# Layer two with the token units outside and the weight sets inside, result sums kept in SBUF, and late weights made one pass earlier

## The chip, the core and the metric

The kernel runs on one core of one Trainium2 chip. The metric is the device time of one execution in microseconds (us). Five engines work side by side, each on its own stream of instructions: PE (TensorE, matmul; PEld is its weight load), DVE (VectorE), ACT (ScalarE), POOL (GpSimd) and SP (SyncE, which here only issues DMAs). ACT and POOL issue DMAs too; such an issue stands in the engine's own stream, so an instruction behind it comes after it. SBUF is the on-chip memory of the engines, PSUM the accumulators of PE, and DRAM everything else.

## The reference

Attention over pooled keys and values, and two gated layers on the 4608 rows of 512 that come out of it. Everything is float32.

```python
def _attn_ref(q, k, v):                 # 8 x 8 heads, 576 long, 64 wide; k and v are means of 8 rows
    scores = scale * np.matmul(q, k_p.transpose(0, 1, 3, 2))
    scores = scores - np.max(scores, axis=-1, keepdims=True)
    attn = np.exp(scores)
    attn = attn / (np.sum(attn, axis=-1, keepdims=True) + 1e-09)
    return np.matmul(attn, v_p).astype(np.float32)

def _moe_ref(x, w_in, w_out):           # "layer one": 4608 x 512, d_ff 2048
    h = x @ w_in
    g = h * (1.0 / (1.0 + np.exp(-1.702 * h)))
    return (g @ w_out).astype(np.float32)

def _moe2_ref(x, w_a, w_b, w_out):      # "layer two": d_ff 1536
    a = x @ w_a
    b = x @ w_b
    return (a * b @ w_out).astype(np.float32)
```

## The kernel before

**Numbers in two halves.** Each float32 factor is split into a rounded part hi and a rest lo, and a product is three matmuls: hi by hi, hi by lo, lo by hi. A split is a copy on ACT (hi) and a subtraction on DVE (lo).

**Blocks, units, passes.** The 4608 tokens are nine blocks of 512. Passes 0 and 1 (attention and the first ten d_ff chunks of layer one) run block by block. From pass 2 the blocks go in five units: units 0 to 3 are two blocks each, unit 4 is the ninth block alone, in two halves of 256. Pass 2 is layer one's last pass; its units come in the order 4, 0, 1, 2, 3. Passes 3, 4 and 5 are layer two: 12 d_ff chunks f in three sets of weights of four chunks, called A, B and C here. From pass 2 each chunk of a unit is made with seven products of half-size matrices in place of eight (`PRODUCTS`), so each unit needs seven operands (three are quarters of the input, `RAW`, and four are differences of quarters, `MIXED`).

**A turn.** A turn is one set of one unit: four chunks of seven products, each of six matmuls (line 784, 168 in all), with a few ACT copies (lines 794 to 798) and DVE steps (from line 800) on each chunk's banks, then the sweep: 14 groups of six matmuls (line 907, 84 in all) that multiply by w_out and whose sums are added into the result (`add_out`: line 954 for a first sum, 956 for the others). A turn's groups run among the next turn's products; `TABLES` says after which product (the O entries). Of a unit of two blocks a matmul has 512 columns, of unit 4 it has 256.

**Order of the turns.** Sets outside, units inside: A0 A1 A2 A3 A4, B0 to B4, C0 to C4 (`steps`, line 1037). The next unit's operands are therefore loaded at each turn, and the sums of a unit leave and come back between its sets:

- Operands. Layer one's result is turned into seven operands (`operand_steps`), all split into hi and lo, that go to DRAM (`yd`, 1 MB each for a unit of two blocks). For units 2 and 3 of pass 2 these steps go one for each product (`PACED`, `results`), for the others all at once. In layer two, `product` issues the load of the next unit's operand (line 417, `load_operand`) on ACT's queue as soon as the last product that reads the old one has been written; the load waits there until the buffer is free. The first unit of a set is loaded by SP.
- Sums. In sets A and B each sum goes to `part[2]` in DRAM, and in B and C it is read back (`load_quarter`, the L entries of `TABLES`, on SP).
- Weights. A set is 28 pieces of w_a and w_b (`wc`, 256 KB each) and 14 of w_out (`wo`, 256 KB each); it is loaded once, by SP.

**Making the weights.** Each chunk of w_a and w_b (a key f) and each pair of chunks of w_out (a key o) is read, combined into seven mixtures, split and stored to DRAM (`wd`) by some tens of small instructions. The first five f keys and three o keys are made in pass 1. The other ten keys (f 5 to 11 and three o) are made in layer two, from A0 to the start of B4 (`made_late`, `pieces_late`): loads and stores on POOL's queue (lines 1224 and 1238), casts on ACT (lines 1134 and 1235), sums on DVE (lines 1135 to 1157, 1236), in tiles called spare and v.

A scheduler puts the instructions of each engine in order from the order in which the code issues them and from their dependences; `tc.issue_after` pins one behind another.

## Time and profile before

| | us |
|---|---|
| median of three runs | 1751.64 |
| lowest and highest of them | 1748.36, 1755.93 |
| the profiled execution | 1749.56 |
| span of its instructions | 1747.7 |
| PE busy | 1700.7 (97%) |
| DVE busy | 1232.7 (71%) |
| ACT busy | 747.3 (43%) |
| POOL busy | 165.7 (9%) |

All steps below are made on the profiled execution, whose time is 1.9 us above its span and 2.1 us below the median. The mean granted TensorE clock was 0.994. The span divides by PE's first product (line 784) of each part: attention and passes 0 and 1 up to 634 us, pass 2 from 634 to 897 us, then the fifteen turns of layer two, A0 from 897 to 956 us and C4 last. A row of the profile names line, engine, operation and tiles (out<-in); the bracket at the end is the idle time of the engine just before, and what ended it.

### The profile page before, as it was taken

To read this page: it belongs to the slowest core of one execution; us is meant where nothing else is said; L and a number is where in the kernel's file an instruction comes from. 1 tells how busy PE (TensorE), PEld (TensorE's weight loads), DVE (VectorE), ACT (ScalarE), POOL (GpSimd) and SP (SyncE) were. 2 spreads that over 40 slices of the span, in tenths; PEclk is the share of its full clock that TensorE was granted. 3 is DMA by queue.
4 is the path that set the end of the run, shared out by engine and by line. 5 is a ranking of instruction groups with operands and counts; after the bars stand their busy time and mean duration, and the time that the engine had idled before them with its cause. 6 is when DMAs were issued, how large, how long until landed. Compare 5 with 4: busy or idle time off the path is not lost.

```text
span 1747.7 us, 24378 instructions
## 1 busy us (share of the span) xinstructions
PE 1700.7 (97%) x8672; PEld 1417.9 (81%) x8672; DVE 1232.7 (71%) x2251; ACT 747.3 (43%) x1782; POOL 165.7 (9%) x282
## 2 busy tenths in 40 slices
PE   9999999999999999999999999999899899999998
PEld 8888887878888888788887777888778787788887
DVE  8999866675868745656637777786778765566666
ACT  8976643543334435455433443443333322222222
POOL 0000000010100001113212211111111100000000
PEclk9999999999999999999999999999999999999999
DMA  7776466465978985476698567499685678734543
GB/s 293 247 270 240 177 209 228 157 229 208 374 276 309 403 320 196 170 272 231 227 403 294 223 259 263 162 358 328 268 331 185 250 270 324 294 126 187 217 157 109
DMA packets 135641, 438.87 MB, mean 251 GB/s; under 512 B 15520, under 2 KB 31392, under 8 KB 114656
## 3 DMA queue, kind: packets, MB, share of 16 engines
q1 hardware_dynamic: 100544, 281.32, 44.5%
q0 software_dynamic: 22880, 78.92, 12.3%
q10 hardware_dynamic: 12096, 77.08, 11.1%
q8 instruction: 68, 1.11, 0.3%
q14 instruction: 53, 0.43, 0.1%
HBM read 291.24 MB, written 146.01 MB: 250 GB/s over the span
## 4 chain that ended last, share of the span: by engine, by line
PE 71%; DMA 11%; DVE 9%; issue 4%; ACT 3%; POOL 1%; SPq 0%; ACTq 0%; POOLq 0%; DVEq 0%
PE X L784 16%; PE acc L907 11%; PE Y L784 8%; PE acc L325 4%; PE acc L326 4%; PE acc L327 4%; PE h L325 4%; PE Z L784 4%; PE h L326 4%; PE h L327 4%; PE acc L715 3%; PE acc L716 3%; PE acc L717 3%; DMA xo<-yd 2%; DMA part<-ys 1%
## 5 line engine op out<-in xcount | busy, mean ns | idle before, releaser
L784 PE MATMUL X<-xo,wc 128*128 128x512 f32 (+1 forms) x1800 | 419.4, 373 | 22.8 <-ACT s L794 10.0
L784 PEld LDWEIGHTS X<-xo,wc 128*128 128x128 f32 x1800 | 319.0, 190 | 86.8 <-ACT s L794 11.1
L784 PE MATMUL Y<-xo,wc 128*128 128x512 f32 (+1 forms) x900 | 210.2, 369 | 5.0 <-DMA xo<-yd 2.5
L784 PEld LDWEIGHTS Y<-xo,wc 128*128 128x128 f32 x900 | 158.4, 188 | 35.5 <-ACT s L796 3.3
L306 ACT CAST ghi<-s 128x512 fp32r<-128x512 f32 (+1 forms) x137 | 79.9, 583 | 243.2 <-PE acc L907 194.8
L907 PE MATMUL acc<-ghi,wo 128*128 128x512 f32 (+1 forms) x548 | 179.1, 372 | 2.0 <-DVE part L956 2.0
L325 PE MATMUL h<-x,w 128*128 128x512 f32 x360 | 144.0, 401 | 2.7 <-ACT x L604 2.2
L326 PE MATMUL h<-x,w 128*128 128x512 f32 x360 | 141.2, 392 | 0.5 <-DVE x L606 0.5
L327 PE MATMUL h<-x,w 128*128 128x512 f32 x360 | 141.1, 392 | 0.0
L326 PE MATMUL acc<-glo,w 128*128 128x512 f32 x360 | 140.3, 390 | 0.2 <-DVE glo L1392 0.2
L327 PE MATMUL acc<-ghi,w 128*128 128x512 f32 x360 | 140.4, 390 | 0.0
L956 DVE TENSOR_TENSOR part<-acc,part 128x512 f32<-128x512 f32 (+1 forms) x170 | 104.9, 634 | 45.8 <-PE acc L907 40.7
L307 DVE TENSOR_TENSOR glo<-s,ghi 128x512 fp32r<-128x512 f32 (+1 forms) x137 | 87.7, 640 | 67.0 <-ACT ghi L306 66.7
L325 PE MATMUL acc<-ghi,w 128*128 128x512 f32 x360 | 131.1, 398 | 0.4 <-ACT ys L1414 0.4
L907 PEld LDWEIGHTS acc<-ghi,wo 128*128 128x128 f32 x548 | 101.9, 189 | 20.6 <-issue 1.9
L794 ACT COPY s<-X 128x512 f32<-128x512 f32 (+1 forms) x75 | 40.8, 543 | 173.5 <-PE X L784 145.1
L784 PE MATMUL Z<-xo,wc 128*128 128x512 f32 (+1 forms) x450 | 105.2, 369 | 0.9 <-DMA xo<-yd 0.7
L907 PE MATMUL acc<-glo,wo 128*128 128x512 f32 (+1 forms) x274 | 101.9, 372 | 0.0
L560 ACT ACTIVATE at<-sc,mx 128x72 f32<-128x72 f32 x288 | 88.2, 341 | 27.5 <-DVE mx L553 27.3
L907 PE MATMUL acc<-hi,wo 128*128 128x512 f32 (+1 forms) x292 | 94.9, 372 | 3.3 <-ACT spare L1235 2.1
L996 POOL DMA_DIRECT2D yd<-st x126 | 67.7, 541 | 269.0 <-ACT st L306 229.4
L784 PEld LDWEIGHTS Z<-xo,wc 128*128 128x128 f32 x450 | 79.7, 189 | 15.8 <-DVE s L814 1.1
(133 smaller groups left out, 3155.2 us busy)
## 6 DMA issues: line engine op xcount, KB each, us to landing
xo<-yd ACTq DMA_DIRECT2D x63, 1024.0 KB, 10.2
part<-part SPq DMA_DIRECT2D x128, 256.0 KB, 3.9
yd<-st POOLq DMA_DIRECT2D x126, 256.0 KB, 3.1
xo<-yd SPq DMA_DIRECT2D x21, 1024.0 KB, 8.3
part<-part SPq DMA_DIRECT2D x19, 1024.0 KB, 8.6
xd<-x SPq DMA_DIRECT2D x18, 1024.0 KB, 7.4
xm<-xd SPq DMA_DIRECT2D x32, 512.0 KB, 8.3
xo<-xd SPq DMA_DIRECT2D x12, 1024.0 KB, 7.7
```

Of the source, the lines that this page charges most:

```text
L306: nc.scalar.copy(out=hi, in_=src)
L307: (nc.vector.tensor_tensor(out=lo, in0=src, in1=f32(hi), op=ALU.subtract))
L325: nc.tensor.matmul(out=o, lhsT=whi, rhs=xhi, start=first, stop=False),
L326: nc.tensor.matmul(out=o, lhsT=whi, rhs=xlo, start=False, stop=False),
L327: nc.tensor.matmul(out=o, lhsT=wlo, rhs=xhi, start=False, stop=last),
L560: pin("ACT", nc.scalar.activation(out=a[:, h, :], in_=sc[:, c, :], func=AF.Exp, bias=mx[:, h:h + 1], accum_out=sm[:, h:h + 1],))
L715: after_last(nc.tensor.matmul(out=oa, lhsT=whi, rhs=chi, start=first, stop=False))
L716: after_last(nc.tensor.matmul(out=oa, lhsT=wlo, rhs=chi, start=False, stop=False))
L784: after_last(nc.tensor.matmul(out=banks[nm], lhsT=w[we][:, ks], rhs=x[:, xe, kk, :], start=n in FIRST and kk == 0 and m == 0, stop=kk == 1 ...
L907: after_last(nc.tensor.matmul(out=o_, lhsT=w_, rhs=x_, start=n in FIRST and k_ % 2 == 0 and m == 0, stop=k_ % 2 == 1 and m == 2, skip_grou ...
L956: nc.vector.tensor_tensor(out=t, in0=a, in1=t, op=ALU.add)
L996: nc.gpsimd.dma_start(out=yd[u][:, o, e, kk] if w_ == N else yd[u][:, o, e], in_=f32(ts[e]))
```

## The change

- **Order of the turns.** Units outside, sets inside, forwards and backwards in turn: A0 B0 C0, C1 B1 A1, A2 B2 C2, C3 B3 A3, A4 B4 C4 (`turns`, `after`). Ten of the fourteen steps from turn to turn change the set, four change the unit.
- **Operands** are loaded once for each unit, by SP, each pinned behind the one before (`last_x`), in place of once in each turn on ACT's queue. Only the three quarters are stored in two halves (1 MB); the four differences are stored unsplit (`ym`, 0.5 MB) and split in layer two by `split_operand`: two in the last chunk of the unit before (behind products 2 and 4), two in the first chunk (behind products 6 and 3).
- **Weights** are loaded anew at each change of set: eleven times in all. The `wc` pieces of chunk n are issued on SP one chunk ahead of the use of their slot, starting in the second chunk of the turn before; the `wo` pieces on POOL's queue within the sweep (the first set's on SP).
- **Sums** of a unit stay in four `part` tiles and one tile of tag wo through its three sets; only the finished ones are stored to the output.
- **Layer one's result.** The steps that make operands come two for each product for all units. A unit of two blocks takes 14 DVE instructions (8 differences, 6 splits) and 6 casts on ACT, in place of 22 and 14.
- **Making of the late weights.** Nine keys (f 6 to 11, three o) in place of ten, begun with pass 2: `tick`, called for each product, issues a share of them over 147 products, of which 105 are pass 2's and 42 the first turn and a half of layer two's; each is pinned behind the last anchored copy or sum. The sixth f key is made in pass 1, and the first two keys (f 0 and o 0) move from pass 1 into the last block of pass 0.
- **Layout.** `wd` holds all hi parts of a key before its lo parts; stores take longer runs, loads two pieces. In pass 2 the second `part` tile takes a slot of tag w in place of v, and SP issues the `part` loads ahead of the operands.

```diff
...
+    turns = []
+    for u in range(NU2):
+        sets = list(range(LP, L2))
+        turns += [(i, u) for i in (sets if u % 2 == 0 else sets[::-1])]
+    after = dict(zip(turns, turns[1:]))
...
-    yd = [dram.tile([P, 7, 2, 2, N if len(u) == 2 else HALF], F32, name=f"yd{n}") for n, u in enumerate(units)]
+    yd = [dram.tile([P, 3, 2, 2, N if len(u) == 2 else HALF], F32, name=f"yd{n}") for n, u in enumerate(units)]
+    ym = [dram.tile([P, 4, 2, N if len(u) == 2 else HALF], F32, name=f"ym{n}") for n, u in enumerate(units)]
...
-    wd = {f: dram.tile([P, 7, 2, 2 * P], F32, name=f"wd{f}") for f in range(NF2)}
+    wd = {f: dram.tile([P, 2, 7, 2 * P], F32, name=f"wd{f}") for f in range(NF2)}
...
-        2: [dram.tile([P, KD, N], F32, name=f"part2_{j}") for j in range(NB)],
...
+        x_t[operand_key(i, u, o)] = t
+        if o in RAW and i >= LP:
             src = yd[u][:, o]
...
+        elif i >= LP:
+            t, src = t[:, 1], ym[u][:, o - 3]
...
-        (queue or nc.sync).dma_start(out=f32(t), in_=src)
+        with tc.issue_after(last_x[0]) if i >= LP and u > 0 else nullcontext():
+            made = nc.sync.dma_start(out=f32(t), in_=src)
+        last_x[:] = [made.ins]
...
-        t = part_t.pop((i, u, col_n, c)) if i < FINISHES else part_t[j][:, c, cols]
+        t = part_t[j][:, c, cols]
...
-            for o in results[:1]:
+            for o in results[:2]:
                 o()
-            del results[:1]
+            del results[:2]
+            tick()
...
-            if last:
-                x_t.pop((i, u, o))
-                if not one_ and u + 1 < NU2:
-                    load_operand(i, u + 1, USED.index(o), nc.scalar)
...
+        ahead = {}
+        if first and (one_ or (i, u) == turns[0]):
+            ahead = {"": (u, 3), "P1": (u, 4), "P6": (u, 5), "P3": (u, 6)}
+        elif first and u != before_[i, u][1]:
+            ahead = {"P6": (u, 5), "P3": (u, 6)}
+        elif last and not one_ and (i, u) in after and after[i, u][1] != u:
+            ahead = {"P2": (u + 1, 3), "P4": (u + 1, 4)}
...
-            if u == NU2 - 1 and i + 1 < L2 and k_ in (3, 7, 11, 13):
-                load_o(i + 1, k_ // 4)
+            if not final and after[i, u][0] != i and k_ in (3, 7, 11, 13):
+                load_o(after[i, u][0], k_ // 4, nc.sync if (i, u) == turns[0] else nc.gpsimd)
...
-            t = part_t[i, u, c, col] = out_tile(c, col, cols.stop - cols.start)
+            n_ = cols.stop - cols.start
+            if col:
+                if (u, "half") not in part_t:
+                    part_t[u, "half"] = big("wo", [P, KD, n_], F32, "sums")
+                t = part_t[u, "half"][:, c]
+            else:
+                t = p2.tile([P, n_], F32, tag="part", name="sum", bufs=4)
+            part_t[u, c, col] = t
...
-        if done:
...
+        if done and after.get((i, u), (0, NU2))[1] != u:
+            part_t.pop((u, c, col))
+            ended.append(op(
+                nc.sync.dma_start, out[c * P:(c + 1) * P, j * N + cols.start:j * N + cols.stop], t
+            ))
...
+        ts = [spare(list(part_.shape), F32R, "st") for _ in range(2)]
...
-        def step(o, out_, a, b, kk):
-            if a is not None:
-                sub(out_, a, b, kk)
-            split_store(u, o, out_, kk)
...
-        todo_ = [(0, b11, None, None), (1, b21, None, None), (2, b22, None, None), (3, b11, b12, b11),
-                 (5, b12, b22, b12), (4, b22, b22, b11), (6, b21, b21, b22)]
-        return [op(step, *x, kk) for x in todo_ for kk in range(2 if b11.shape[-1] == N else 1)]
...
+            return a[:, kk] if wide else a
+        def mixture(o, a, b, kk):
+            a, b = (t[x, kk] if isinstance(x, int) else cut(x, kk) for x in (a, b))
+            t[o, kk] = spare(list(a.shape), F32, "mix")
+            nc.vector.tensor_tensor(out=t[o, kk], in0=a, in1=b, op=ALU.subtract)
+            nc.gpsimd.dma_start(out=ym[u][:, o - 3, kk] if wide else ym[u][:, o - 3], in_=t[o, kk])
+        ks = range(2 if wide else 1)
+        def chained(kk):
+            mixture(3, b12, b11, kk)
+            mixture(4, b22, 3, kk)
+            mixture(6, b21, 4, kk)
+        todo_ = [(chained,), (mixture, 5, b22, b12), (split_store, u, 2, b22), (split_store, u, 0, b11),
+                 (split_store, u, 1, b21)]
+        return [op(*x, kk) for kk in ks for x in todo_]
...
-        steps_ = operand_steps(u, *q4)
-        if u in PACED:
-            results.extend(steps_)
-        else:
-            for o in steps_:
-                o()
+        results.extend(operand_steps(u, *q4))
...
-    steps = [(i, j, f) for i in range(len(passes)) for j in order[i] for f in chunks(i, j)]
+    steps = [(i, j, f) for i in range(LP) for j in order[i] for f in chunks(i, j)]
+    steps += [(i, u, f) for i, u in turns for f in passes[i][1]]
...
-    HELD, EARLY = FM - FA, FB + 1
+    HELD, EARLY = FM - FA, FB + 2
...
+    def tick():
+        if not background:
+            return
+        pace[0] += 1
+        while background and background[0][0] <= pace[0]:
+            _, o = background.pop(0)
+            with ExitStack() as pinned:
+                for ins in anchored.values():
+                    pinned.enter_context(tc.issue_after(ins))
+                o()
+    def in_background(ops, ticks):
+        total, done = sum(o.cost for o in ops), 0.
+        for o in ops:
+            background.append((2 + ticks * done / total, o))
+            done += o.cost
...
-    spread_late(mixed_x(3) + made_p(2), place[0, J9, 1], place[0, J9, FM - 1])
+    spread_late(mixed_x(3) + made_p(2) + made([0]), place[0, J9, 1], place[0, J9, FM - 1])
     J5 = order[1][-1]
     spread_late(
-        mixed_x(4) + made(range(EARLY)),
+        mixed_x(4) + made(range(1, EARLY)),
...
-    spread_late(
-        made_late(range(EARLY, NF2)), place[LP, 0, passes[LP][1][1]], place[L2 - 2, NU2 - 1, passes[L2 - 2][1][0]] - 3,
...
+    for u, next_ in zip(order[i], order[i][1:] + [None]):
+        homes = ("wo", "w") if len(units[u]) == 2 else ("w",)
+        parts = [op(load_part, j, t) for j, t in zip(units[u][::-1], homes)]
+        if next_ is not None:
+            before.setdefault((i, u, fs[1]), []).extend(parts + operands(i, next_))
...
+            before.setdefault((i, u, fs[0]), []).extend(parts + loads(LP))
+    before[LP, 0, passes[LP][1][1]] = [op(load_o, LP, m, nc.sync) for m in range(4)]
+    for (i, u), (i2, u2) in after.items():
+        fs, fs2 = passes[i][1], passes[i2][1]
+        if u2 != u:
+            before.setdefault((i, u, fs[-1]), []).extend(operands(LP, u2))
+        if i2 != i:
+            for n, f in enumerate(fs2):
+                key = (i, u, fs[n + 1]) if n + 1 < FB else (i2, u2, fs2[0])
+                before.setdefault(key, []).extend(ab_ops(i2, f))
...
```

ACT at a change of unit in layer two, before (B0 to B1; xo is an operand and yd1 its place in DRAM, s a chunk's sums, hi and ghi rounded halves, v a weight being made):

```order
L798 COPY s_11363<-X_11324 128x512
L954 COPY part_11368<-acc_10946 128x256
L306 CAST hi_11407<-s_11218 128x512
L954 COPY part_11373<-acc_10950 128x256
L306 CAST ghi_11434<-s_10936 128x512
L417 DMA xo_11390<-yd1_92 128x2048
L417 DMA xo_11403<-yd1_92 128x2048
L417 DMA xo_11417<-yd1_92 128x2048
L417 DMA xo_11430<-yd1_92 128x2048
L794 COPY s_11461<-X_11452 128x512
L796 COPY s_11469<-Y_11453 128x512
L1134 ACTIVATE v_11180<-spare_11188 128x256
```

and now (C0 to C1):

```order
L804 COPY s_10135<-Y_10113 128x512
L806 COPY s_10143<-X_10112 128x512
L311 CAST hi_10176<-s_10014 128x512
L311 CAST ghi_10199<-s_9785 128x512
L435 CAST xo_10100<-xo_10100 128x1024
L435 CAST xo_10102<-xo_10102 128x1024
L802 COPY s_10212<-X_10203 128x512
L804 COPY s_10220<-Y_10204 128x512
L311 CAST ghi_10231<-s_10014 128x512
L806 COPY s_10241<-X_10203 128x512
L311 CAST hi_10253<-s_9913 128x512
L435 CAST xo_10106<-xo_10106 128x1024
```

The four loads that stood between a turn's last cast and the next turn's first copy `s` are gone from ACT; two casts that split operands of the next unit stand there instead, and two more behind the first copies.

SP in set B, before (`part` are sums in SBUF, part2 their place in DRAM):

```order
L612 DMA part2_0_134<-part_11380 128x512
L612 DMA part2_0_134<-part_11382 128x512
L947 DMA part_11685<-part2_0_134 128x512
L947 DMA part_11687<-part2_0_134 128x512
L612 DMA part2_1_135<-part_11420 128x512
L612 DMA part2_1_135<-part_11422 128x512
L947 DMA part_11800<-part2_3_137 128x512
L947 DMA part_11802<-part2_3_137 128x512
L612 DMA part2_1_135<-part_11297 128x512
L612 DMA part2_1_135<-part_11299 128x512
L947 DMA part_11918<-part2_3_137 128x512
L947 DMA part_11920<-part2_3_137 128x512
```

and now, in unit 1's turns (wc is a set's weights, wd their place in DRAM):

```order
L1305 DMA wc_10620<-wd7_113 128x2x1024
L1305 DMA wc_10735<-wd0_106 128x2x1024
L1305 DMA wc_10737<-wd0_106 128x2x768
L1305 DMA wc_10737<-wd1_107 128x2x256
L1305 DMA wc_10849<-wd1_107 128x2x1024
L1305 DMA wc_10851<-wd1_107 128x2x512
L1305 DMA wc_10851<-wd2_108 128x2x512
L1305 DMA wc_10957<-wd2_108 128x2x1024
L1305 DMA wc_10959<-wd2_108 128x2x256
L1305 DMA wc_10959<-wd3_109 128x2x768
L1305 DMA wc_11051<-wd3_109 128x2x1024
L430 DMA xo_11377<-ym2_98 128x1024
```

The stores and loads of sums are gone from SP, and loads of weights stand there, with the next unit's operands behind them.

DVE in pass 2, before, where a unit's operands are made (part is layer one's result, st a half to be stored, glo a rest):

```order
L800 TENSOR_TENSOR s_6969<-s_6969,Y_6897 128x512
L730 TENSOR_TENSOR part_6686<-acc_6977,part_6686 128x512
L767 TENSOR_TENSOR glo_6996<-s_6969,ghi_6995 128x512
L307 TENSOR_TENSOR st_7082<-part_6686,st_7081 128x512
L1001 TENSOR_TENSOR part_6686<-part_6680,part_6686 128x512
L809 TENSOR_TENSOR s_6949<-s_6949,X_6896 128x512
L1001 TENSOR_TENSOR part_6680<-part_6680 128x512
L307 TENSOR_TENSOR st_7100<-part_6680,st_7099 128x512
L730 TENSOR_TENSOR part_6686<-acc_7011,part_6686 128x512
L767 TENSOR_TENSOR glo_7027<-s_6949,ghi_7026 128x512
L1001 TENSOR_TENSOR part_6680<-part_6680,part_6686 128x512
L307 TENSOR_TENSOR st_7088<-part_6686,st_7087 128x512
```

and now (v and raw are a weight being made):

```order
L808 TENSOR_TENSOR s_7149<-s_7149,Y_7070 128x512
L1138 TENSOR_SCALAR v_6932<-v_6932 128x256
L1137 TENSOR_SCALAR v_6932<-v_6932 128x256
L1141 SCALAR_TENSOR_TENSOR v_6932<-raw_6977,v_6932 128x256
L1138 TENSOR_SCALAR v_6932<-v_6932 128x256
L1144 TENSOR_SCALAR raw_6977<-v_6932 128x256
L1141 SCALAR_TENSOR_TENSOR v_6932<-raw_7033,v_6932 128x256
L743 TENSOR_TENSOR part_6779<-acc_7157,part_6779 128x512
L1145 SCALAR_TENSOR_TENSOR raw_6977<-raw_6977 128x256
L778 TENSOR_TENSOR glo_7180<-s_7149,ghi_7179 128x512
L1144 TENSOR_SCALAR raw_7033<-v_6932 128x256
L1148 TENSOR_TENSOR v_6932<-v_6932,raw_6977 128x256
```

Between the same two steps of a chunk (lines 800 and 767 before, 808 and 778 now), where one sum stood, stand that sum and seven small instructions that make weights.

## Rows read from the trace of the kernel before

**Rows 1.** Page: busy time, share of the span, instructions of each engine.

```profile
PE 1700.7 (97%) x8672; PEld 1417.9 (81%) x8672; DVE 1232.7 (71%) x2251; ACT 747.3 (43%) x1782; POOL 165.7 (9%) x282
```

**Rows 2.** Turns A1 to B3, C0 to C2: start:end, length, busy (instructions), clock, DMA share, GB/s.

```profile
core 0: us, PE busy (x) PEld busy (x) DVE busy (x) ACT busy (x) POOL busy (x), PEclk, DMA share, GB/s
955.61:1022.47 66.86, 60.10 (x253) 48.08 (x253) 46.98 (x101) 25.43 (x48) 11.41 (x19) 0.97 0.66 249
1022.47:1079.62 57.15, 57.15 (x254) 47.30 (x252) 46.56 (x97) 24.88 (x46) 13.64 (x21) 1.00 0.62 225
1079.62:1140.64 61.02, 58.05 (x254) 46.93 (x252) 44.72 (x97) 23.85 (x45) 9.25 (x15) 1.00 0.62 231
1140.64:1180.16 39.52, 39.52 (x253) 35.91 (x252) 32.82 (x76) 19.19 (x41) 7.63 (x12) 1.00 0.97 359
1180.16:1229.40 49.24, 48.76 (x254) 41.50 (x253) 35.71 (x82) 18.12 (x42) 7.64 (x12) 1.00 0.92 337
1229.40:1297.66 68.26, 61.25 (x254) 49.37 (x252) 52.47 (x108) 20.88 (x40) 14.19 (x22) 0.95 0.71 267
1297.66:1360.03 62.37, 57.90 (x253) 47.06 (x252) 48.96 (x102) 20.04 (x37) 8.71 (x14) 1.00 0.69 255
1360.03:1418.70 58.67, 57.83 (x253) 47.07 (x252) 43.80 (x76) 17.64 (x31) 5.47 (x8) 1.00 0.63 233
...
1458.61:1512.82 54.21, 50.10 (x255) 42.66 (x253) 26.62 (x54) 11.99 (x25) 0.00 (x0) 0.97 0.74 278
1512.82:1575.04 62.22, 59.07 (x254) 48.39 (x252) 38.13 (x59) 15.76 (x27) 0.00 (x0) 0.97 0.54 202
1575.04:1632.16 57.12, 57.12 (x254) 47.30 (x252) 36.80 (x57) 15.35 (x26) 0.00 (x0) 1.00 0.53 200
```

**Rows 3.** The same view of pass 2, and of 50 us near pass 0's end.

```profile
634.18:897.43 263.25, 262.37 (x1282) 222.03 (x1281) 154.61 (x236) 133.48 (x232) 53.03 (x99) 1.00 0.65 239
...
455.00:505.00 50.00, 50.00 (x223) 41.38 (x222) 33.75 (x63) 19.72 (x30) 2.65 (x4) 1.00 0.85 323
```

**Rows 4.** Timeline of ACT at the change from B0 to B1: start, length, instruction.

```profile
1224.75 10.99 ACTq L417 DMA_DIRECT2D xo<-yd  x4
1235.78 0.58 ACT L794 COPY s<-X 128x512 f32<-128x512 f32 x1 [10.59 <-DMA wo<-wdo]
```

**Rows 5.** Timeline of PE at the same place.

```profile
1230.77 1.52 PE L784 MATMUL Y<-xo,wc 128*128 128x512 f32 x6
...
1236.42 1.43 PE L784 MATMUL X<-xo,wc 128*128 128x512 f32 x4 [2.78 <-ACT s L794]
```

**Rows 6.** Timeline of ACT at two steps of the late weights.

```profile
1289.35 0.41 ACT L1235 CAST spare<-v 128x256 fp32r<-128x256 f32 x1 [4.51 <-DMA wdo<-spare]
...
1356.33 0.43 ACT L1134 ACTIVATE v<-spare 128x256 f32<-128x256 f32 x1 [5.30 <-DMA spare<-in_moe_w_a_dram]
```

**Rows 7.** Timeline of PE at three such places.

```profile
1251.28 0.47 PE L907 MATMUL acc<-hi,wo 128*128 128x512 f32 x1 [2.06 <-ACT spare L1235]
...
1290.43 0.50 PE L784 MATMUL Y<-xo,wc 128*128 128x512 f32 x1 [2.18 <-ACT s L796]
...
1358.54 0.73 PE L784 MATMUL X<-xo,wc 128*128 128x512 f32 x2 [3.58 <-DVE s L814]
```

**Rows 8.** Turns A1 to B4: all work on tile v, then line 1143 alone.

```profile
core 0: us, DVE busy (x) ACT busy (x) POOL busy (x), PEclk, DMA share, GB/s
955.61:1458.61 503.00, 103.30 (x280) 39.26 (x80) 27.27 (x40) 0.99 0.72 268
...
955.61:1458.61 503.00, 16.60 (x40) 0.99 0.72 268
```

**Rows 9.** Groups by line: busy, mean ns | idle before them, and what ended it.

```profile
L1235 ACT CAST spare<-v 128x512 fp32r<-128x512 f32 (+1 forms) x40 | 22.5, 568 | 30.1 <-DMA wdo<-spare 9.3 <-DMA wd<-spare 8.2 <-DVE v L1146 6.6
L1134 ACT ACTIVATE v<-spare 128x256 f32<-128x256 f32 x40 | 17.0, 434 | 26.4 <-DMA spare<-in_moe_w_out_dram 7.5 <-DMA wd<-v 6.5 <-DMA spare<-in_moe_w_a_dram 6.0
L1236 DVE TENSOR_TENSOR v<-v,spare 128x512 fp32r<-128x512 f32 (+1 forms) x40 | 24.2, 619 | 8.7 <-ACT spare L1235 8.4
L422 DVE TENSOR_TENSOR xo<-xo 128x1024 fp32r<-128x1024 f32 (+1 forms) x20 | 22.3, 1116 | 19.0 <-ACT xo L421 19.0
L421 ACT CAST xo<-xo 128x1024 fp32r<-128x1024 f32 (+1 forms) x20 | 19.3, 964 | 11.4 <-DMA xo<-xc 11.3
```

**Rows 10.** DMA issues: count, KB each, median us from issue to landing.

```profile
xo<-yd SPq DMA_DIRECT2D x21, 1024.0 KB, 8.3
...
wc<-wd SPq DMA_DIRECT2D x12, 1024.0 KB, 12.2
...
xo<-xc SPq DMA_DIRECT2D x16, 512.0 KB, 6.5
```

221 lines of the change are left out of this document (86 added, 135 removed), and 6 rows, old and new, of tables (ENDING, TABLES).

## The prediction

> **What bounds the kernel now.** I read the page first: PE is busy 97% of the span [rows 1], so nothing is won by making another engine faster as such; only idle time of PE, or its matmuls, can shorten the run. The change keeps all matmuls of layer two. So the question is where PE loses time and whether the change touches it. Next I cut layer two at PE's first product of each turn [rows 2]. In C2 PE is busy for the whole 57.12 us: that is the floor of a turn of a unit of two blocks with a wide sweep behind it. B0, with unit 4's narrow sweep in it, has 49.24 us and C0 should have the same; A4, narrow products with a wide sweep, takes 39.52 us with PE never idle. Against these floors the turns lose: A1 66.86 - 57.12 = 9.74; A2 nothing; A3 61.02 - 57.12 = 3.90; B1 68.26 - 57.12 = 11.14; B2 62.37 - 57.12 = 5.25; B3 58.67 - 57.12 = 1.55; C0 54.21 - 49.24 = 4.97; C1 62.22 - 57.12 = 5.10. Together 41.65, with the small rests of the turns not shown some 42 us. Pass 2 loses nothing that matters: 262.37 of 263.25 us busy [rows 3]. So the most that the change can win in layer two is 42 us, and everything that it adds can only take from that.
>
> **What causes the 42 us.** The third view is the timeline at the costliest place, B0 to B1. Four issues of operand loads stand in ACT's queue and take 10.99 us there, for each waits until the old operand's buffer is free; the copy of the first product's bank, which PE needs to go on, stands behind them, and ACT starts it only after 10.59 us of idleness, at 1235.78 [rows 4]. PE's next products follow it at 1236.42, 2.78 us idle [rows 5]. The bracket names a DMA of wo as the releaser, but the row above it says what ACT was doing. A second cause stands in B1 to B3: casts of the late weights wait 4.51 and 5.30 us on ACT for a DMA [rows 6], and what stands behind them reaches PE late, 2.06 + 2.18 + 3.58 = 7.8 us [rows 7]. So I put about 34 us down to the operand loads on ACT and 8 to the late weights.
>
> **The change, part by part.** All from the profiled 1749.56.
>
> *Operand loads leave ACT: minus 34 us.* The waiting issues go from ACT altogether; on SP they wait too, but nothing that PE needs at once stands behind them there except weights that are wanted about three quarters of a turn later. There are four changes of unit in place of twelve inside the sets.
>
> *What a change of unit costs now.* An operand's buffer is free when its last product ends. A product or a group is six matmuls; 252 of them take 57.12 us, so one takes 0.227 and six 1.36. In the last chunk the first product is followed by six more products and two groups, 8 x 1.36 = 10.9 us, before the next unit's first product wants its operand; 1 MB on SP lands in 8.3, 0.5 MB in about 6.5 [rows 10], and the operands that come unsplit need a cast and a subtraction more, 0.96 + 1.12 = 2.1 us [rows 9]. It fits by 1 to 3 us, if SP issues at once. Lower bound zero: A2 and C2 took seven whole operands without loss [rows 2]. Upper bound 5.1 each: C1, where no late weights are made. The four changes of set C lost 5.1, 0, 0 and next to nothing, 1.4 in the mean; I take 1.0, since 5 MB come in place of 7 and ACT is free: 4 x 1.0 = plus 4 us (0 to 20).
>
> *Ten changes of set.* Each brings 10.5 MB of weights. A load lands 12.2 us after its issue [rows 10], and it is issued three chunks ahead, 3/4 of 57.12 = 43 us; 11.0 million bytes in 57.12 us are 193 GB/s, where A4 ran at 359 [rows 2]. What is taken away is larger: per turn 7 MB of operands and the sums, both ways. I cost the changes at nothing; the cover is those 43 us. If it fails, the price is C0's, the one change of set that lost: 4.97 each (0 to 50).
>
> *Unit 4's turns.* B4 has narrow products and a narrow sweep: 39.52 - (57.12 - 49.24) = 31.6 us. The set for C4 has to come in this time: 11.0 million bytes at 359 GB/s are 30.7 us, at B1's 267 they are 41.2. Between 0 and 41.2 - 31.6 = 9.6 late; I take 2, near the first, since nothing else is loaded there.
>
> *Late weights, now mostly in pass 2.* In layer two the ten keys took 103.30 + 16.60 = 119.9 us of DVE and 39.3 of ACT [rows 8]; nine are 108 and 35. 105 of the 147 products over which they are spread are pass 2's: 71%, 77 us of DVE and 25 of ACT. The units of two blocks save 8 DVE instructions each, 32 x 0.62 (line 1236's 512 columns [rows 9]) = 20 us. DVE in pass 2 goes to 154.6 + 77 - 20 = 212 of 263 us, 80%, ACT to some 155. A2 had DVE at 46.56 of 57.15, 81%, with late weights in it and no loss [rows 2]. So the load is carried; what stays is waits at the head of a queue. What is queued behind such a wait on ACT are the copies of banks X and Y and the casts of the gate's halves, and PE waits for these. Lower bound 0; upper bound all of ACT's idle time before the two lines, (30.1 + 26.4) x 9/10 = 50.9 us [rows 9], if none of it were hidden. Before, 7.8 us of it reached PE for ten keys, 0.78 each; I take the same for nine, plus 7, since the instructions and their waits are the same and now pinned behind the copies instead of ahead of them.
>
> *Sums in SBUF, layout, early keys.* The sums' stores and loads were on SP and nobody waited for them in C2; with them gone the adds cost as before: 0. The sixth f key goes to passes 0 and 1 and two move into pass 0's last block; at its end PE is never idle with DVE at 33.75 of 50.00 us [rows 3], so one key (12 us of DVE) is covered: plus 1 (0 to 7.8, the three stalls of rows 7). In pass 2 five units' operand steps come two for each product, 14 instructions in place of 22: hidden as before, 0.
>
> **Sum.** 1749.56 - 42 + 4 + 0 + 2 + 7 + 1 = 1721.6. The profiled execution lies 2.1 below the median of 1751.64, so 1723.7, say 1723.
>
> **Rivals.**
>
> R1, *the stalls belong to the transfers, not to ACT's queue.* Then moving the issue wins little at the four changes that are left, and they cost what inside-set changes cost before, from 2.4 us (the mean of A1 to A4's and C1 to C4's, 19.1/8) to 5.1. For it: the profile's bracket names a DMA [rows 4]. Against it: the copy waits for no DMA's data, and C2 took 7 MB with no loss. It gives 1721.6 + 4 x 1.4 = 1727 up to 1721.6 + 4 x 4.1 = 1738. The Trainium skill, in "DMA: Bandwidth & Descriptors", section "Issuing engines are not separate DMA queues", says that DMAs issued by scalar, sync or gpsimd run on the same 16 engines and that spreading the issue saves only the sequencer's time to initiate, usually small. By that rule the move from ACT to SP would win nearly nothing of itself; the row of 10.99 us for four issues disagrees, because the wait for a free buffer is the sequencer's time too.
>
> R2, *slower: the head-of-line waits of the late weights are exposed in pass 2.* The mechanism is one: a cast of a late weight waits on ACT (or DVE) for its DMA while copies of product banks stand behind it, in a pass that before lost nothing and where DVE goes from 59% to 80%. Price up to 50.9. With all of it exposed 1723 - 7 + 51 = 1767. It decides from the point at which 7 + 28 + 8.7 = 44 us are exposed (slower by over 0.5%, which is 8.7 us and about what a measurement can tell); from 27 us on the gain is within 0.5%.
>
> R3, *the last unit becomes bound by DMA*: B4 and C4 each wait the 9.6 us worked out above: 1723 - 2 + 2 x 9.6 = 1740.
>
> R4, *slower: sets arrive late at every change of set* because SP's or POOL's queue holds their issue (POOL's behind stores of late weights, SP's behind an operand that waits for its buffer): 10 x 4.97 = 50 more, 1773. Against it: SP's weights stand ahead of the operands in its order, and the late weights end in the second turn, B0.
>
> **How the numbers follow.** Forecast as summed, with its terms between their bounds: 0.57 (0.54 faster, 0.03 within 0.5%, if several terms go to their upper ends). R1 0.12 and R3 0.07, both still faster. R2 0.20 (0.07 slower, 0.10 within, 0.03 still faster). R4 0.04 (0.03 slower, 0.01 within). With all losses gone and nothing added the time is 1749.56 - 42 = 1707.6, and the median may be as low against it as the lowest run shows: 1706 is the low end. The high end takes in R1 and R3 and part of R2: 1746. Faster by over 0.5%: 0.76; within: 0.14; slower: 0.10.
>
> **What would show it.** Right: turns of units 0 to 3 at 57 to 58 us, no operand issue on ACT, PE idle at the changes of unit under 2 us each, pass 2 at 263 to 270 us with DVE near 212. R1: 3 to 5 us of idle PE at three or four changes of unit, with the operand's DMA as releaser. R2: pass 2 longer by over 20 us, with lines of the late weights as releasers and idle DVE or ACT before them. R3: B4 and C4 over 40 us with DMA share above 0.9. R4: idle PE at each first chunk with wc or wo as releaser. I would be wrong altogether if the matmuls themselves were more or slower (PE busy other than about 1701 us, or the clock below 0.99).

## The result

The changed kernel takes 1721.54 us, the median of six runs (1718.5 to 1723.66), against 1749.38 us for the kernel before (six runs, 1747.38 to 1755.93). The ratio is 0.9836, with a 95% interval from 0.9817 to 0.9854: 1.6% faster. The forecast was 1723, the range 1706 to 1746. The profiled execution has a span of 1719.3 us, 28.4 less than before. The number was hit; of its terms several were not, and it was luck that they made up for each other. The rest of this document is about that.

The page of the changed kernel, busy time of each engine, answers to [rows 1]:

```profile
PE 1689.5 (98%) x8672; PEld 1415.3 (82%) x8672; DVE 1232.2 (72%) x2221; ACT 746.0 (43%) x1762; POOL 205.3 (12%) x371
```

PE has the same 8672 matmuls and is busy 11.2 us less. So of the 28.4 us only 17 are idle time that went. The mean granted clock rose from 0.994 to 0.999, by estimate some 8 to 9 us over the span, so most of the 11.2 is matmuls that run at a higher clock (below); where the rest comes from is not shown.

The turns of the changed kernel in their new order, A0 B0 C0 C1 B1 A1 A2 C2 C3 A3 and unit 4's three, with the columns of [rows 2]:

```profile
core 0: us, PE busy (x) PEld busy (x) DVE busy (x) ACT busy (x) POOL busy (x), PEclk, DMA share, GB/s
900.67:958.72 58.05, 57.03 (x250) 46.58 (x249) 41.49 (x79) 18.47 (x33) 12.48 (x23) 1.00 0.96 362
958.72:1016.20 57.48, 57.42 (x254) 47.22 (x253) 43.05 (x85) 23.71 (x44) 10.87 (x18) 1.00 0.70 255
1016.20:1073.36 57.16, 57.16 (x253) 47.30 (x252) 45.56 (x89) 19.91 (x36) 16.28 (x28) 1.00 0.67 246
1073.36:1132.34 58.98, 57.52 (x253) 47.16 (x252) 42.13 (x62) 18.47 (x30) 0.00 (x0) 1.00 0.55 198
1132.34:1189.64 57.30, 57.30 (x254) 47.23 (x252) 31.71 (x49) 19.26 (x34) 7.46 (x14) 1.00 0.54 194
1189.64:1250.10 60.46, 57.74 (x254) 47.16 (x253) 38.44 (x59) 17.30 (x29) 7.46 (x14) 1.00 0.43 146
1250.10:1307.21 57.11, 57.11 (x253) 47.30 (x252) 38.78 (x59) 16.93 (x28) 0.00 (x0) 1.00 0.49 167
...
1364.49:1425.86 61.37, 58.05 (x254) 47.66 (x252) 38.06 (x58) 17.36 (x28) 7.47 (x14) 0.99 0.39 142
1425.86:1484.10 58.24, 58.24 (x253) 47.95 (x252) 39.32 (x60) 17.16 (x28) 0.00 (x0) 0.98 0.49 166
...
1541.38:1601.60 60.22, 57.44 (x254) 47.22 (x253) 37.86 (x60) 17.49 (x30) 7.46 (x14) 1.00 0.38 131
1601.60:1641.12 39.52, 39.52 (x253) 35.92 (x252) 29.62 (x58) 12.13 (x26) 0.00 (x0) 1.00 0.67 238
1641.12:1671.43 30.31, 30.31 (x255) 30.30 (x253) 17.84 (x48) 11.95 (x34) 7.46 (x14) 1.00 0.91 326
1671.43:1719.30 47.87, 42.33 (x338) 40.77 (x336) 31.96 (x88) 13.67 (x37) 7.46 (x14) 0.99 0.32 109
```

Two things are to be seen. Where only the set changes (B0, C0, B1, and the turns left out), a turn takes 57.1 to 57.5 us, the floor of 57.12. And the loss that is left sits at the four changes of unit: 1.86 (C1), 3.34 (A1, at its end), 4.25 and 1.12 (C2 and C3), 3.10 (A3, at its end), 13.7 us in all. Pass 2 went from 263.25 to 265.71 us, the part ahead of it from 634.18 to 634.96.

Where the 13.7 us come from is seen at C2 to C3. First ACT, then DVE, then PE:

```profile
1420.80 1.04 ACT L435 CAST xo<-xo 128x1024 fp32r<-128x1024 f32 x1 [3.74 <-DMA xo<-ym]
```
```profile
1421.88 1.23 DVE L436 TENSOR_TENSOR xo<-xo 128x1024 fp32r<-128x1024 f32 x1 [2.47 <-ACT xo L435]
1423.02 0.68 DVE L821 TENSOR_TENSOR s<-s,X 128x512 f32<-128x512 f32 x1
```
```profile
1423.75 4.60 PE L796 MATMUL X<-xo,wc 128*128 128x512 f32 x12 [3.32 <-DVE s L821]
```

The split of an operand that comes unsplit waits on ACT for its DMA. Its subtraction waits on DVE for the cast, and the sum of line 821, which sets PE's bank X free, stands behind it. PE had all its operands for product 4 and waited 3.32 us for that sum. It is a wait at the head of a queue, of the kind that the prediction feared for the late weights, at a place where it had only asked whether the operand comes in time.

### The profile page after: what moved, and what is told of

Its sections match the earlier page's. It is cut to its first block, busy times and chain, and to the rows that moved or that the text cites. A ratio compares the mean times of both kernels' runs of the same rounds, so it can differ in the third digit from the quotient of the medians.

```text
span 1719.3 us, 24087 instructions
## 1 busy us (share of the span) xinstructions
PE 1689.5 (98%) x8672; PEld 1415.3 (82%) x8672; DVE 1232.2 (72%) x2221; ACT 746.0 (43%) x1762; POOL 205.3 (12%) x371
## 4 chain that ended last, share of the span: by engine, by line
PE 40%; issue 4%; DMA 3%; DVE 2%; POOL 1%; ACT 0%; SPq 0%; POOLq 0%; DVEq 0%; ACTq 0%
PE X L796 15%; PE acc L916 14%; PE Y L796 7%; PE Z L796 3%; DMA xo<-ym 2%; DMA ym<-mix 0%; DMA wdo<-hi 0%; PE acc L728 0%; PE acc L729 0%; PE acc L730 0%; POOL wd L1240 0%; ACT xo L435 0%; DVE xo L436 0%; DVE s L821 0%; POOL yd L993 0%
## 5 line engine op out<-in xcount | busy, mean ns | idle before, releaser
L796 PEld LDWEIGHTS X<-xo,wc 128*128 128x128 f32 x1800 | 318.0, 189 | 72.4 <-DVE s L821 11.2
L942 POOL DMA_DIRECT2D wo<-wdo x126 | 67.3, 540 | 589.0 <-PE acc L916 561.1
L973 DVE TENSOR_TENSOR sums<-acc,sums 128x512 f32<-128x512 f32 (+1 forms) x100 | 61.9, 636 | 42.4 <-PE acc L916 42.4
```

The costliest lines, as they stand in the source:

```text
L796: after_last(nc.tensor.matmul(out=banks[nm], lhsT=w[we][:, ks], rhs=x[:, xe, kk, :], start=n in FIRST and kk == 0 and m == 0, stop=kk == 1 ...
L942: queue.dma_start(out=f32(t_), in_=wd["o", passes[i][1][0] // 2 + k_ % 2][:, PRODUCTS[SWEEP[k_ // 2]][0]])
L973: nc.vector.tensor_tensor(out=t, in0=a, in1=t, op=ALU.add)
```

## The experiments

Each kernel was timed beside the kernel before on its chip; the ratio is to that, so 0.9836 is the changed kernel and 1 the one before.

| run | edit, in short | median us | ratio (95%) |
|---|---|---|---|
| b_sp_queue | before, operands issued by SP | 1738.83 | 0.9918 (0.9900 to 0.9935) |
| b_no_late | before, no late weights made | 1739.60 | 0.9931 (0.9903 to 0.9959) |
| b_sp_no_late | both | 1728.26 | 0.9865 (0.9841 to 0.9889) |
| b_wo_pool | before, wo loads on POOL | 1750.27 | 0.9981 (0.9963 to 0.9999) |
| e_act_queue | changed, operands issued by ACT | 1720.57 | 0.9818 (0.9798 to 0.9837) |
| e_reload | changed, operands anew at each turn | 1771.25 | 1.0110 (1.0079 to 1.0141) |
| e_split_pinned | changed, splits moved and pinned behind copies and sums | 1714.56 | 0.9776 (0.9751 to 0.9800) |
| e_no_making | changed, no late weights made | 1718.14 | 0.9810 (0.9781 to 0.9839) |
| e_forward | changed, sets always A B C | 1722.18 | 0.9835 (0.9804 to 0.9867) |
| e_dense | changed, late weights over 70 products | 1716.47 | 0.9789 (0.9765 to 0.9814) |
| e_no_late | changed, copies in place of late weights | 1744.85 | 0.9948 (0.9932 to 0.9964) |
| e_double | changed, each wc load followed by a copy within DRAM | 1845.80 | 1.0530 (1.0509 to 1.0551) |

### Is it ACT's queue? b_sp_queue and e_act_queue

```diff
-                    load_operand(i, u + 1, USED.index(o), nc.scalar)
+                    load_operand(i, u + 1, USED.index(o))
```

> The kernel before, with one edit: the next unit's operands are issued by SP in place of ACT; the order of turns, the sums in DRAM and the late weights stay. Theory (the stall is the issue that waits in ACT's queue ahead of a copy): of the 42 us that the turns lose, the losses at the changes of unit go down by 20 to 34 us, to 1716 to 1730 us, and no copy of a bank waits 10 us on ACT. Rival R1 (the transfer itself is late): nothing moves, 1745 to 1752 us, and the releaser of the first product is the operand's DMA. A third outcome: SP's queue, where loads of sums now stand behind operands that wait for a buffer, gives part of it back; then DVE adds to sums wait for the part DMA.

It gave 0.8%, some 14 us, and not 20 to 34. What PE waits for in layer two (the first lines of each view), the kernel before and then this one:

```profile
PE X L784 <- ACT s L794: 10.0, 3, 4.1
PE X L784 <- DMA xo<-yd: 6.7, 5, 2.0
PE X L784 <- DVE s L814: 5.9, 5, 3.6
PE Y L784 <- DMA xo<-yd: 2.5, 2, 1.9
```
```profile
PE X L784 <- DMA xo<-yd: 7.3, 7, 2.3
PE Y L784 <- DMA xo<-yd: 5.9, 4, 2.1
PE acc L907 <- DVE part L956: 5.4, 8, 2.3
```

The columns are us in total, times and longest. The copy of bank X, late on ACT for 10.0 us, is gone from the list, and the waits for the operand's own DMA grew from 9.2 to 13.2 us. Behind the wait that was taken away stood, in part, the transfer. Nor did the gain come where the prediction had read the mechanism. Turns B1 and C0 of this run, with the columns of [rows 2]:

```profile
1226.09:1294.60 68.51, 62.05 (x254) 48.96 (x253) 51.88 (x108) 21.27 (x40) 13.89 (x22) 0.95 0.69 253
1456.32:1504.80 48.48, 48.48 (x255) 41.58 (x254) 27.55 (x56) 12.88 (x26) 0.00 (x0) 1.00 0.81 299
```

B1 is as long as before, 68.51 against 68.26 us. C0, the turn behind a change of set, went from 54.21 to 48.48: 5.7 of the 8.9 us by which the profiled span is shorter.

```diff
-            made = nc.sync.dma_start(out=f32(t), in_=src)
+            made = (nc.scalar if i >= LP and u > 0 else nc.sync).dma_start(out=f32(t), in_=src)
```

> The changed kernel, with one edit: in layer two the operands of units 1 to 4 are issued on ACT in place of SP. Theory: each of the four changes of unit costs 5 to 11 us, as B1 and C1 did before, in place of some 3: 1730 to 1752 us, with a copy of a bank on ACT that starts late behind the issues. R1: 1719 to 1724 us, since only the issuer differs.

No difference from the changed kernel: R1's number, not mine. So an operand issue on ACT is not costly by itself. What it costs depends on what it waits for. In the trace many of the loads have a row that waits for a semaphore just before their issue. The rows at B0 to B1 in the kernel before, worked out from the trace's list of instructions (time of the issue, how long ACT stood there, the semaphore, and the DMA that had last used it):

```
1230.14  4.90  S100  xo<-yd, issued by ACT at 1221.29
1232.09  1.56  S102  wo<-wdo, issued by SP at 1223.36
1235.42  2.95  S103  wo<-wdo, issued by SP at 1223.72
```

SP and ACT share eight such semaphores, POOL has eight others, and an issue waits until the DMA that last raised its semaphore has landed. So the bracket of [rows 4], "10.59 <-DMA wo<-wdo", was right, and the prediction set it aside: the last product on the old operands had begun before B1's first, at 1229.40 [rows 2], and the three semaphores were raised at 1230.07, 1232.01 and 1235.34. Over layer two ACT stood 33.6 us at such semaphores in the kernel before, nearly all of it from B0 to B1, in C0, and from C0 to C1 (the longest, 10.08 us up to 1465.26 in C0, for a load of wc); with ACT issuing in the changed kernel it is 0.1 us, with SP issuing 1.4. What the prediction called waits for a free buffer were, at B0 to B1, waits for earlier DMAs to land. At the other places no row tells when the buffer came free, so how much ACT would have waited there without the semaphores is not shown.

The Trainium skill, "DMA: Bandwidth & Descriptors", section "Issuing engines are not separate DMA queues", says that the DMAs of the scalar, sync and gpsimd engines run on the same 16 DMA engines and that starting them on several engines saves only the sequencer's time to initiate them, usually small. e_act_queue agrees, with 1720.57 against 1721.54 us; b_sp_queue does not, with its 14 us, since there the issuer stood waiting with copies behind it.

### b_wo_pool: are the semaphores the bound?

```diff
-            nc.sync.dma_start(
+            nc.gpsimd.dma_start(
```

(in `load_o`)

> The kernel before, with one edit: the loads of w_out (wo, 42 in layer two) are issued on POOL in place of SP. In the trace of before, SP and ACT share eight semaphores for their DMAs, POOL has eight others; an issue waits until the DMA that last used its semaphore has landed, and two of the waits at B0 to B1 (1.56 and 2.95 us) are for wo loads. Theory (the long waits on ACT are for these semaphores, not for operands' buffers): the waits on wo go, B1 loses 3 to 6 us less than its 11: 1743 to 1748 us where before has 1751, and ACT's wait for semaphores in layer two falls well under 33 us. Rival (the DMAs themselves are late, whoever issues them): no change in B1, 1749 to 1753 us.

The measurement falls between: 0.2%, some 3 us, and the interval just leaves out no change. B1 fell from 68.26 to 65.08 us as expected. But B2 went from 62.37 to 66.00, PE's waits for copies of bank X from 10.0 to 11.1 us, and ACT's time at the semaphores did not fall: 21.1 us counted as above, and 4.88 and 7.52 us more in two rows that wait for two such semaphores at once, from 1221.90 and 1289.07 on, each until a DMA had landed; 33.5 in all. The waits on wo went, and waits for other DMAs of SP and ACT took their place. That the semaphores hand on a stall whose cause is the transfers fits this; it is not shown.

### Late weights: b_no_late, b_sp_no_late, e_no_making

```diff
-                out=f32(t[:, k_ % 4]), in_=wd["o", passes[i][1][0] // 2 + k_ % 2][:, PRODUCTS[SWEEP[k_ // 2]][0]]
+                out=f32(t[:, k_ % 4]), in_=wd["o", (passes[i][1][0] // 2 + k_ % 2) % 3][:, PRODUCTS[SWEEP[k_ // 2]][0]]
...
-        key = ("h", f) if passes[i][0] == 3 else f
+        key = ("h", f) if passes[i][0] == 3 else f % 5
...
-    spread_late(
-        made_late(range(EARLY, NF2)), place[LP, 0, passes[LP][1][1]], place[L2 - 2, NU2 - 1, passes[L2 - 2][1][0]] - 3,
-    )
```

> The kernel before without the making of the ten late weights: the sets of layer two read early weights again in their place, so as many bytes come in, but the weights are wrong ones and some 120 us of DVE and 39 us of ACT work are left out. Theory (the late weights cost layer two the 8 us of PE time that the trace shows directly): 1740 to 1744 us. Rival (their instructions also push others back, so they cost more than the waits that name them): 1730 to 1738 us. The loss of B1 with its waits for semaphores should stay in part.

Some 12 us (1 - 0.9931 of 1754), between the two: the three stalls that the trace names made 7.8; that the rest is work pushed back is argued. B1 takes 60.17 us here in place of 68.26, so of the 11 us that it lost, which the prediction read as operand loads on ACT, some 8 go with the late weights (5 with SP as issuer: 68.51 to 63.14).

> As the run without late weights, and the operands are issued by SP in place of ACT. The issuer alone gave some 14 us, the late weights should give 8 or more. If the two are separate costs, both add: 1725 to 1732 us. If they are the same stalls seen from two sides, less than the sum: 1733 to 1738 us. What is left above some 1710 us then belongs to the operands' transfers at twelve changes of unit.

Some 24 us, nearly the sum of 14.4 and 12.1. They are separate costs. Of the kernel before's losses 24 us are then accounted for by the issuer and the late weights. What is left is not spread over the changes of unit. A1, B1 and C1 of this run, with the columns of [rows 2], and PE's two longest waits in layer two:

```profile
958.18:1020.53 62.35, 58.69 (x254) 46.75 (x252) 34.04 (x52) 20.37 (x36) 2.70 (x5) 1.00 0.59 227
1224.01:1287.15 63.14, 58.50 (x253) 46.91 (x252) 36.90 (x57) 15.34 (x26) 0.00 (x0) 1.00 0.55 207
1490.77:1552.32 61.55, 59.05 (x253) 48.39 (x252) 37.01 (x58) 15.24 (x26) 0.00 (x0) 0.97 0.57 213
```
```profile
PE X L784 <- DMA xo<-yd: 6.9, 7, 2.5
PE Y L784 <- DMA xo<-yd: 4.2, 3, 1.5
```

These three, the turns behind the first change of unit in each set, lose 15.7 us against 57.12; A2, A3, B2, B3, C2 and C3 together lose 2.2. PE's waits name the operand's DMA. Why it is late there and hardly at the others no run tells; that the sums go to DRAM and back there is a rival that was not tried alone.

The same edit in the changed kernel (`f % 6`, and no `in_background`):

> The changed kernel without the making of the nine late weights: the sets read early weights again in their place, the same bytes but wrong weights; some 108 us of DVE and 35 us of ACT work are left out, and nothing is issued instead. It replaces the run whose copies ran at another place than meant. Theory: the late weights cost 3 to 7 us in pass 2 and the first turn: 1714 to 1719 us. Rival: nothing measurable, 1720 to 1723 us.

The ratio is 0.0026 lower than the changed kernel's, 4.6 us, though the intervals overlap; the span is 0.5 us lower. So making nine keys costs the changed kernel some 0 to 5 us, and ten cost the one before 12.

### e_reload: how much is the number of changes?

```diff
-        return min(i, LP), u, o
+        return i, u, o
...
-        if u2 != u:
-            before.setdefault((i, u, fs[-1]), []).extend(operands(LP, u2))
+        before.setdefault((i, u, fs[-1]), []).extend(operands(i2, u2))
```

(and the splits at each turn, each operand of a unit of two blocks in a slot of tag w)

> The changed kernel, but with the operands loaded and split anew at each of the fourteen steps from turn to turn in place of the four changes of unit; order of turns, sums in SBUF, weights and late weights as in the changed kernel. It doubles what comes in within a turn (10.5 MB of weights and 5 MB of operands). Theory (the gain comes from having four changes of operands in place of twelve): each of the ten more costs what the four cost, about 3.4 us: 1745 to 1760 us. Rival (the gain came from the sums and the late weights that left these turns, and loading operands is cheap by itself): under 1.5 us each, 1722 to 1735 us.

It takes 1771.25 us, 50 more than the changed kernel: ten more changes of operands at 5 us each, slower than the kernel before. The order of turns, the sums in SBUF and the late weights are still as the change made them, so the gain hangs on having few changes of operands beside the loads of sets. PE's waits in layer two:

```profile
PE X L796 <- DVE s L821: 20.5, 10, 4.5
PE X L796 <- DMA xo<-yd: 6.7, 2, 3.5
PE X L796 <- DVE xo L436: 5.3, 5, 2.0
```

Most of what is named here are sums behind a split, not the operand's DMA. The kernel before loaded its operands split, and most of its turns brought no set; so the 5 us are the price of a change in the changed kernel, and not that of its twelve.

### e_split_pinned: the new wait, taken away

```diff
-            ahead = {"P6": (u, 5), "P3": (u, 6)}
+            ahead = {"": (u, 5), "P6": (u, 6)}
...
-            ahead = {"P2": (u + 1, 3), "P4": (u + 1, 4)}
+            ahead = {"P7": (u + 1, 3), "P4": (u + 1, 4)}
...
-                split_operand(i, *ahead[what])
+                with ExitStack() as pinned:
+                    if not one_ and (i, u) != turns[0]:
+                        for ins in anchored.values():
+                            pinned.enter_context(tc.issue_after(ins))
+                    split_operand(i, *ahead[what])
```

> The changed kernel, with one edit: at a change of unit the four splits of operands (cast on ACT, subtraction on DVE) are pinned behind the copies and sums of the products before them, so that none of them waits for its DMA ahead of the sum that sets bank X free. Theory of the trace: at three of the four changes PE waits 1.7 to 3.3 us for that sum because a subtraction that waits for its operand stands ahead of it on DVE; with the pin these go, minus 5 to 9 us: 1712 to 1717. Rival: the operand's transfer is late anyway and PE waits for the operand itself instead: 1719 to 1723 us, with xo as the releaser of the next unit's second product.

The edit moves the splits to other products and pins them. 1714.56 us, ratio 0.9776: faster than the changed kernel, with intervals that don't touch. PE's waits in layer two for the changed kernel, and for this one:

```profile
PE X L796 <- DVE s L821: 7.8, 3, 3.3
PE acc L916 <- issue: 1.6, 4, 0.8
PE X L796 <- DVE xo L436: 1.5, 1, 1.5
```
```profile
PE acc L920 <- issue: 1.6, 4, 0.8
PE X L796 <- DVE xo L436: 1.5, 1, 1.5
...
PE X L796 <- DVE s L821: 0.4, 1, 0.4
```

The wait for line 821's sum went from 7.8 to 0.4 us and no wait for the operand's DMA took its place. The turns that had lost 13.7 us lose 3.8. The transfer was in time; the order on DVE was not.

### e_forward: what a change of set costs

```diff
-        turns += [(i, u) for i in (sets if u % 2 == 0 else sets[::-1])]
+        turns += [(i, u) for i in sets]
```

> The changed kernel, with the sets always in the order A B C: fourteen changes of set in place of ten, and each change of unit is a change of set as well. Theory (a change of set costs 0.2 us, a change of unit 3): within 2 us of 1721 in the turns of units 0 to 3, somewhat more at a change of unit, where operands now stand behind the next set's weights: 1721 to 1732 us. Rival (the two together fill the DMA engines or SP's queue): 5 to 10 us at each of four changes, 1741 to 1760 us.

No difference: 0.9835 against 0.9836, with an interval that leaves room for some 5 us. Fourteen changes of set cost what ten did, that is, next to nothing, and going forwards and backwards in turn is not what brings the gain.

### e_dense: late weights closer together

```diff
-    in_background(made_late(range(EARLY, NF2)), 7 * (FP * NU2 + 2 * FB - 2))
+    in_background(made_late(range(EARLY, NF2)), 70)
```

> The changed kernel, with the nine late weights spread over 70 products in place of 147: all of them fall into the first ten of pass 2's fifteen chunks. Without them DVE is busy about half of pass 2 (134.95 of 270 us); with all of them in two thirds of it DVE comes to its full share there. Theory (it is carried as long as DVE has room, and costs a few waits): plus 5 to 25 us, 1726 to 1747 us, with DVE above 0.9 in these chunks. Rival (waits at the queue's head, not DVE's share, set the cost, and they are as many as before): within 3 us of 1721.

It came out 5 us faster than the changed kernel, which neither theory had. It did not do what it says: pass 2 holds 195.37 us of DVE work here, 195.83 in the changed kernel, so no more of the making fell into it. The numbers of `tick` give the earliest place; what set the pace in their place is not shown. The run says nothing on how much DVE can carry, and where its 5 us come from stays open (C1 took 57.17 us in place of 58.98, A0 56.75 in place of 58.05).

### Two that went to another place: e_no_late and e_double

```diff
+            nc.gpsimd.dma_start(out=wd[key][c * 64:(c + 1) * 64], in_=wd[like][c * 64:(c + 1) * 64])
```

(in place of `load`, `make` and `store` of `pieces_late`)

> The changed kernel without the making of the nine late weights: in their place POOL issues two copies of early weights in DRAM for each, so layer two computes with wrong weights of the same amount. It leaves out about 108 us of DVE and 35 us of ACT work. Theory: these cost 3 to 7 us of PE time, so 1714 to 1719 us, nearly all of it in pass 2 and the first turn. Rival R2 (head-of-line waits of the late weights cost more, 10 us and up): 1711 us or less.

It was slower by 23 us than the changed kernel, though work was left out. The copies depend on nothing but an early weight, and the scheduler put them ahead, at 493 to 660 us, into passes 0 and 1. Stretches 500 to 600 us and up to the start of the units of two blocks, this kernel and then the changed one:

```profile
500.00:600.00 100.00, 90.72 (x383) 72.92 (x383) 62.82 (x115) 35.37 (x54) 4.86 (x10) 0.95 0.94 357
600.00:690.00 90.00, 79.32 (x422) 67.88 (x421) 44.02 (x83) 31.42 (x63) 2.97 (x6) 0.94 1.00 383
```
```profile
500.00:600.00 100.00, 100.00 (x443) 82.81 (x442) 81.45 (x150) 40.33 (x63) 0.00 (x0) 1.00 0.93 350
600.00:664.00 64.00, 61.50 (x356) 54.11 (x356) 32.26 (x69) 26.80 (x57) 2.17 (x4) 1.00 0.89 324
```

In the changed kernel DMA is busy 0.93 there already, at 350 GB/s. PE waited 15.0 us in these stretches for loads of x, and not at all for them in the changed kernel's. e_no_making was run in its place.

```diff
+            if not isinstance(key, tuple):
+                nc.sync.dma_start(out=twice[key][:, :, c:c + n], in_=stored(key, c, c + n))
```

> The changed kernel, with each load of a w_a and w_b piece in layer two followed on SP by a copy of the same piece within DRAM, which nobody reads: 7 MB more read and 7 MB more written for each set. Theory (ten changes of set are free since the weights are issued some 40 us ahead and the DMA engines have room): turns of units 0 to 3 stay within 1 us of 57.1 to 57.3, while B4 and C4, whose 30 us just hold their set, get longer by 5 to 20 us: 1727 to 1745 us. Rival (no room): each change of set loses 3 us or more, 1750 us and up.

1845.80 us, past both. Again the copies, which wait for no slot, ran early: all 110 were issued between 500 and 1200 us. The turns after that are those of the changed kernel, so the question of room for a change of set is not answered. What it does show is a deadline. Turns C0 and C1 of this run, and PE's first two waits in them:

```profile
1065.45:1160.26 94.81, 65.56 (x253) 52.07 (x252) 57.76 (x123) 23.72 (x44) 13.04 (x24) 0.84 0.73 263
1160.26:1257.16 96.90, 62.80 (x253) 50.55 (x252) 60.27 (x111) 24.56 (x42) 20.65 (x34) 0.81 0.63 223
```
```profile
PE acc L917 <- DMA wo<-wdo: 33.4, 2, 20.8
PE X L797 <- DMA wc<-wd: 15.8, 1, 15.8
```

The late weights were made late: the last f key is stored at 1132 us and the last o key at 1201, and set C, which begins at 1065, was not there for its first two turns. In the changed kernel the last f key is stored at 972 us and C0 begins at 1016; the last o key is stored at 1059.

## Why the prediction came out right, point by point

- **What bounds the kernel, and the 42 us: mis-sized.** The floor of a turn with unit 4's narrow sweep was too high. The changed kernel has a turn of narrow products with a narrow sweep, 30.31 us, where I had worked out 31.6: the sweep's difference is 39.52 - 30.31 = 9.21, not 7.88. Measured by that, B0 and C0 of the kernel before lost 1.3 us more each, and its end some 1.3 more: 46 us in place of 42. (Not all of it is waiting: b_sp_queue's C0, with PE never idle, takes 48.48 us, 0.6 above the 47.9 that this floor gives.)
- **PE busy other than about 1701 us as the sign of being "wrong altogether": that sentence was wrong.** The same matmuls took 1689.5 us. Of the turns with losses in [rows 2], A1, B1 and C1 had the clock at 0.95 to 0.97 and PE busy 59 to 61 us in place of 57.15. A closer window of the kernel before, from the stall at B0 to B1 on:

```profile
1231.00:1236.00 5.00, 2.65 (x12) 1.87 (x10) 0.00 (x0) 0.22 (x1) 0.00 (x0) 1.00 1.03 422
1236.00:1240.00 4.00, 3.58 (x10) 2.87 (x11) 2.37 (x7) 2.79 (x6) 0.00 (x0) 0.65 1.02 418
1240.00:1244.00 4.00, 4.00 (x17) 3.22 (x17) 3.31 (x7) 1.48 (x3) 0.72 (x1) 0.92 1.02 418
1244.00:1249.00 5.00, 5.00 (x24) 3.98 (x22) 4.97 (x12) 0.62 (x1) 0.74 (x1) 1.00 0.67 260
1249.00:1254.00 5.00, 2.94 (x14) 2.31 (x13) 5.00 (x10) 2.06 (x4) 2.09 (x3) 1.00 0.17 61
1254.00:1260.00 6.00, 6.00 (x29) 4.95 (x28) 4.79 (x9) 2.90 (x5) 3.00 (x6) 1.00 0.73 238
```

  PE was idle for about half of five microseconds, and over the next four the granted clock was 0.65 in the mean, a mixture of its two levels, 2.4 and 1.2 GHz. Ten matmuls were begun in those 4 us, against 24 in the 5 us from 1244 on at full clock. After this stall the idle microseconds are only part of its cost. Not after each: PE was idle for 2.06 us from 1249 to 1254, and the clock stayed at 1.00. The 42 held this, since it was read from the length of the turns.
- **"About 34 us to the operand loads on ACT and 8 to the late weights": the step that failed.** The issuer is worth 14 us (b_sp_queue) and the late weights 12 (b_no_late), and at B0 to B1, from which the step was read, the profiled turn lost as much with SP as issuer, and 5 to 8 us less without late weights. Of the remaining 46 - 24 = 22 or so, b_sp_no_late places 15.7 in the turns behind the first change of unit in each set, with waits for the operand's DMA; their cause stays open. For the kernel before R1 was nearer in this, and e_act_queue finds the issuer without weight in the changed kernel. In the changed kernel R1's price is met and not its mechanism: its sign was the operand's DMA as releaser, and PE waited for a sum behind a split.
- **"4 x 1.0" for the changes of unit: too small.** They cost 13.7, 3.4 each, inside the bounds of 0 to 20 and R1's price; the sign "under 2 us each" of idle PE failed, with 3.32 at C2. The working took the cast and the subtraction as 2.1 us between landing and use, and did not ask what is queued behind them on DVE while they wait. That had been asked for the late weights alone.
- **Changes of set at nothing: held.** 0 to 0.4 us each, and e_forward with fourteen gives the same time.
- **Unit 4's turns, 2 us: 0.** B4 ran at its floor with DMA share 0.91 and 326 GB/s. R3 did not happen.
- **Late weights, 7 us: 0 to 5.** Pass 2 got 2.5 us longer, of which 1.3 is one wait. That it is the late weights that lengthen it is not shown: without them, in e_no_making, pass 2 takes 269.98 us. The stretch of pass 2 in the changed kernel:

```profile
634.96:900.67 265.71, 263.16 (x1283) 222.31 (x1281) 195.83 (x397) 137.12 (x249) 77.80 (x142) 1.00 0.76 271
```

  DVE is at 195.83 us, 74%, where I had 212 and 80%. Without late weights it is 137.11 (e_no_making), so the 20 us saved were 17.5, and 59 us of the making fell here in place of 77. R2 did not happen.
- **Early keys, plus 1: 0.8.** R4 did not happen in the changed kernel; e_double shows what a set that comes late looks like.

Summed anew for the span: -46 + 13.7 + 2.5 + 0.8, and 1 for the changes of set, is -28.0, against the -28.4 measured. The forecast's -28 was the same number from -42 + 14: the loss was 4 us larger, the changes of unit cost 10 more, and the late weights and unit 4 some 6 less. That these cancel was luck.

## What to carry to other kernels

Count how often operands are changed, and ask what else comes in beside them, before asking who loads them: in the changed kernel ten more changes, beside the sets and with their splits, cost 50 us; in the kernel before, without late weights and with SP as issuer, 15.7 us sat behind three of its twelve changes; and the issuer was worth 0 or 14, depending on what the issue waits for. When the profile's bracket names a DMA, follow that DMA, even if the row above it seems to explain the wait. And a step that consumes a transfer (a cast, a subtraction) belongs in the queue behind whatever PE waits for next: moving and pinning them at four changes of unit won some 7 us, and no wait for a transfer took their place.
